# Retention in two-batch steps with routing in three rounds, in a retention-and-experts kernel

## Chip, cores and metric

The kernel runs on one core of a Trainium2 chip, as one launch. The metric is device time in microseconds (us); lower is better. Before the change the median of three runs is 463.68 us (463.49 to 468.06).

## What is computed

A retention layer feeds a mixture of experts. Arrays are float32: 4 batches, 8 heads, 768 positions, 64 features a head; so 3072 tokens of 512 features, 8 experts of 1024 hidden units.

```
for t in range(S):                       # retention, S = 768
    state = gamma * state + outer(k[t], v[t])
    y[t] = scale * (q[t] @ state)
x = y as rows (3072, 512)
logits = x @ w_gate                      # (3072, 8)
expert = argmax(logits); gate = softmax(logits)[expert]
out[row] = gate * (relu(x[row] @ w1[expert]) @ w2[expert])
```

The kernel uses the chunked form of retention. For 128 positions it computes scores (queries times keys, masked to the causal half), the product of the scores with the values, and, from the second chunk on, the product of the queries with a running state of 64x64 per head.

## The kernel before

Four engines follow an order written out by hand: TensorE (PE), VectorE (DVE), ScalarE (ACT) and GpSimd (POOL). SyncE (SP) issues nearly all transfers, in the order in which the program names them. Each engine works through its list without overtaking, so an instruction that waits holds all behind it on its engine.

**Retention, units of one batch.** `steps` (L453) lists 24 units, a unit being one chunk of one batch: for each pair of chunks, for each batch, the even and then the odd chunk. One query tile holds both chunks of a pair, so queries are loaded, scaled and transposed for every second unit. `load` (L456) runs five units ahead on SP, with six buffers for keys and for values. `scale` (L478) multiplies queries and values by decay factors, on POOL except for the first unit. `transpose` (L499) turns keys and queries on PE, and ACT copies them out (L513, L516). `retain` (L520) does a unit: the scores (L528) on PE, their masking on DVE (L530, tile `am`), then for the next unit the transposes, the new state (PE L539, DVE L542), the query-state product (L556), the product of scores and values (L560), and three copies of the result into `xTg` on ACT (L563, L567; for the last unit two of them on DVE, L569). `to_rows` (L571) turns a unit into rows on DVE (L574); `store` (L579) writes four units to the scratch `x_d` with four transfers of 256 KB (L581).

**Routing, six rounds.** After every four units `place` (L584) is started. It is a generator: each `next(rest)` in the loop puts its next piece into the engines' lists. It computes the logits (PE L591), picks each token's expert, ranks the tokens within an expert (PE L624 to L628, `rk`), and builds with one-hot products (`val` L662, `here` L670, PE `found` L677) the table `inv` (L680) of which token stands in which place. The fifth round, after 20 of the 24 units, ends with `sources` (L173) and a gather of the first 256 rows of experts 0 and 1 from `x_d` (L166, POOL): the early rows. The sixth is spread over the first expert's first layer.

**Between retention and the experts.** DVE copies the early rows of expert 0 (`xe`, L741), PE transposes them (L754), and they are copied out as `xTa` (L756, L758). Then come the eight blocks of the first layer for 256 rows (`layer1`, L223; `hTa`), among which the last round's pieces stand (after blocks 0, 1 and 3; `count`, L415, after block 2). The second layer of the early rows is `pair` (L341), a scheme with seven products instead of eight, which needs sums of the hidden values (`halves_of_h`, L248: `he`, two on DVE and two on POOL) and of the weights (`halves_of_w`, L259: `we`, four on DVE). Two of the weight sums stand before the first layer in DVE's list (L760), two after the last round (L772). After that DVE transposes the other rows of expert 0 (`xTa`, L209) and all of expert 1 (`xT1`, L786), and the loop over the experts (L899) starts. It is a chain of PE work to the end.

**Buffers in PSUM.** Eight banks: two for scores (`sc`), one for logits (`lg`), three for transposes, new state and routing (`tr`), two for outputs (`y`).

Of the kernel before, what the change touches and what calls it, by code (L numbers as in the profile page):

```python
# [53 lines left out]
def kernel(  # L54
# [24 lines left out]
    FAR = 1 << 20  # L79
    assert NC == S // P and D == 64 and DM == H * D and N == B * S and NT == B * NC and DM == 512  # L80
# [51 lines left out]
    nc.gpsimd.iota(tile_4, pattern=[[Q, NT]], base=1, channel_multiplier=0, **exact)  # L132
# [6 lines left out]
    acc = rt([P, NC + 1, E], "acc", BF16)  # L139
# [43 lines left out]
    def targets(got, far, name):  # L183
# [5 lines left out]
        nc.vector.tensor_single_scalar(two, at, 2 * Q - 1, op=ALU.bitwise_and)  # L189
        nc.vector.tensor_single_scalar(bt, at, (2 * Q).bit_length() - 1, op=ALU.arith_shift_right)  # L190
        nc.vector.tensor_single_scalar(bt, bt, B - 1, op=ALU.bitwise_and)
        nc.vector.tensor_single_scalar(ct, at, (2 * Q * B).bit_length() - 1, op=ALU.arith_shift_right)
        nc.vector.scalar_tensor_tensor(out=far, in0=two, scalar=float(L), in1=far, op0=ALU.mult, op1=ALU.add)
        nc.vector.scalar_tensor_tensor(out=far, in0=ct, scalar=float(2 * P), in1=far, op0=ALU.mult, op1=ALU.add)
# [220 lines left out]
    def count():  # L415

        cnt = ps("y", 2, "cnt")[:, 0:E]
        nc.tensor.matmul(cnt, lhsT=ones_b, rhs=acc[:, NC, :], start=True, stop=True)
        ne = rt([P, E], "ne")
        nc.vector.tensor_copy(ne, cnt)  # L420
        return ne
# [14 lines left out]
    with ExitStack() as actx:  # L436
# [6 lines left out]
        def warm(width):  # L443
            nc.tensor.matmul(ps("lg", 1, "warm")[:, 0:width], lhsT=idle[:, 0:P], rhs=idle[:, 0:width], start=True, stop=True)
# [6 lines left out]
        xg = [keep.tile([P, B, Q, DT * L], F32, tag=f"xg{i}", name=f"xg{i}") for i in range(2)]  # L451
        xTg = [keep.tile([P, DT, B, P], F32, tag=f"xTg{i}", name=f"xTg{i}") for i in range(2)]
        steps = [(2 * m + e, b) for m in range(NC // 2) for b in range(B) for e in range(2)]  # L453
        qkv, scaled, qT2, front, state = {}, {}, {}, {}, {}

        def load(n):  # L456
            c, b = steps[n]
            got = {}
            for nm, src in (("k", k), ("q", q), ("v", v)) if n else (("q", q), ("k", k), ("v", v)):
                if nm != "q":  # L460
                    got[nm] = att.tile([P, H, D], F32, tag=nm, name=nm, bufs=6)
                    nc.sync.dma_start(got[nm], src[b, :, ts(c, P), :].rearrange("h t d -> t h d"))
                elif c % 2 == 0:
                    got[nm] = att.tile([P, H, 2 * D], F32, tag=nm, name=nm, bufs=3)
                    for hs in (range(2) if n == 0 else [0]):
                        part = ts(hs, HP) if n == 0 else slice(0, H)
                        nc.sync.dma_start(got[nm][:, part, :], src[b, part, ts(c // 2, 2 * P), :].rearrange(
                            "h (t e) d -> t h (e d)", e=2))
            qkv[n] = got

        def heads_first(src, pairs=range(HP), tr=None):
            if tr is None:
                tr = ps("tr", 3, "tr").rearrange("p (a t) -> p a t", a=HP)
            for a in pairs:
                nc.tensor.transpose(tr[:, a, :], src[:, 2 * a : 2 * a + 2, :].rearrange("p h d -> p (h d)"), ident)
            return tr

        def scale(n):  # L478
            c, b = steps[n]
            got = qkv.pop(n)  # L480
            mul = nc.gpsimd if n else nc.vector
            qs = None
            if c % 2 == 0:
                qs = att.tile([P, 2, H, D], F32, tag="qs", name="qs")
# [10 lines left out]
            if n:  # L495
                scale_v()
# [498 lines left out]
```

## Time and profile before

| | |
|---|---|
| three runs | 463.49, 463.68, 468.06 us |
| the profiled execution | 468.13 us, its span 466.4 us |
| mean granted TensorE clock | 0.992 |
| PE busy | 443.3 us, 95% of the span |
| DVE busy | 295.1 us, 63% |
| POOL busy | 244.0 us, 52% |
| ACT busy | 130.5 us, 28% |
| moved by DMA | 72.75 MB, mean 156 GB/s |

A row of the timeline has the start in us from the start of the span, the duration, the engine, the line, the operation, out<-in, the shapes, how many instructions are merged in the row, and in brackets how long the engine had been idle before it and what it had waited for. A table of windows has for each stretch the busy time of each engine with its instructions, the clock that the throttle granted TensorE (PEclk), the busy share of the DMA engines, and what they moved.

### The profile page before, as it was taken

Reading aid. Unit: us, or ns where it says so; the run is one execution under the profiler, and the core shown is the slowest. Engines: PE = TensorE matmul, PEld = TensorE weight load, DVE = VectorE, ACT = ScalarE, POOL = GpSimd, SP = SyncE. Lnnn points to the kernel's source line nnn. Section 1 sums busy time; section 2 is a strip of 40 time slices with the busy share of each in tenths; the row PEclk is TensorE's granted clock in tenths of the full one; section 3 lists DMA queues with packets and bytes.
Section 4 is the critical chain, followed back from the end, with each engine's and each line's share of the span. In section 5 each row is a group of like instructions: output and inputs, shape, how many; then the busy total and the mean of one; then the engine's idle time right before and its main releaser. Section 6 shows DMA issues by size and latency. Waiting matters only on the chain.

```text
span 466.4 us, 9449 instructions
## 1 busy us (share of the span) xinstructions
PE 443.3 (95%) x3550; PEld 354.6 (76%) x3550; DVE 295.1 (63%) x674; ACT 130.5 (28%) x315; POOL 244.0 (52%) x192
## 2 busy tenths in 40 slices
PE   8899999989799999999999999999989999999992
PEld 4778777767567774558977994898889599699772
DVE  4468788798677792842676567257766748744410
ACT  3454444535322020221231132114213212212310
POOL 3772624450304247728924890885389189179311
PEclk9999999999989999999999999999999999999998
DMA  9998999998931089605804532290562415001001
GB/s 202 225 239 202 220 214 225 241 222 268 288 91 42 4 301 386 245 13 215 273 4 183 174 152 82 107 313 7 185 229 87 180 50 214 5 6 63 4 28 49
DMA packets 93543, 72.75 MB, mean 156 GB/s; under 512 B 53482, under 2 KB 78058, under 8 KB 93424
## 3 DMA queue, kind: packets, MB, share of 16 engines
q1 hardware_dynamic: 88160, 58.74, 44.9%
q0 software_dynamic: 5120, 12.60, 7.6%
q8 instruction: 47, 0.77, 0.7%
q14 instruction: 72, 0.59, 0.4%
q10 hardware_dynamic: 144, 0.05, 0.0%
HBM read 60.88 MB, written 14.68 MB: 162 GB/s over the span
## 4 chain that ended last, share of the span: by engine, by line
PE 59%; DVE 5%; issue 1%; ACT 0%; POOLq 0%; DVEq 0%
PE p L303 24%; PE p L349 18%; PE p L236 13%; PE p L223 5%; DVE xT L209 2%; DVE xTa L209 1%; DVE xs L355 0%; PE yp L349 0%; POOLq L991 0%; ACT o L241 0%; ACT o L242 0%; DVE u L355 0%; DVE hT L307 0%; DVE two L189 0%; DVE dst L195 0%
## 5 line engine op out<-in xcount | busy, mean ns | idle before, releaser
L236 PE MATMUL p<-w2t,hT 128*8 128x128 f32 (+6 forms) x496 | 66.5, 361 | 0.0
L236 PEld LDWEIGHTS p<-w2t,hT 128*8 128x8 f32 (+6 forms) x496 | 32.2, 122 | 30.0 <-issue 26.7
L209 DVE STREAM_TRANSPOSE xT<-xs 32x512 f32<-32x512 f32 x64 | 44.9, 702 | 6.2 <-issue 5.1
L394 POOL DMA_INDIRECT out_dram<-o,dst x30 | 29.9, 996 | 28.3 <-ACT o L244 11.8
L166 POOL DMA_INDIRECT xs<-x_d,src x28 | 29.3, 1045 | 29.2 <-DVE gate_e L201 18.0
L530 DVE TENSOR_TENSOR am<-sc,causal 128x512 f32<-128x512 f32 x48 | 30.7, 681 | 17.2 <-PE sc L528 13.7
L209 DVE STREAM_TRANSPOSE xTs<-xs 32x512 f32<-32x512 f32 x48 | 33.7, 702 | 12.1 <-issue 11.3
L487 POOL TENSOR_TENSOR qs<-q,dec 128x512 f32<-128x512 f32 x22 | 22.5, 1044 | 35.0 <-DMA q<-in_q_dram 33.9
L954 POOL COPY turn_of<-t 128x1 f32<-128x1 f32 x6 | 1.1, 182 | 74.2 <-DVE t L289 74.2
L349 PE MATMUL p<-ws,hs 128*128 128x256 f32 x168 | 37.4, 379 | 0.0
L307 DVE TENSOR_TENSOR hT<-p,q 128x196 f32<-128x196 f32 (+5 forms) x72 | 23.9, 359 | 20.8 <-PE p L303 20.0
L303 PE MATMUL p<-t,w1t 128*128 128x196 f32 (+5 forms) x192 | 35.8, 329 | 0.0
L303 PE MATMUL p<-t,s 128*128 128x196 f32 (+5 forms) x192 | 35.8, 329 | 0.0
L349 PEld LDWEIGHTS p<-ws,hs 128*128 128x128 f32 x168 | 31.9, 190 | 4.3
L492 POOL TENSOR_TENSOR vs<-v,dec 128x512 f32<-128x512 f32 x23 | 23.9, 1042 | 21.4 <-DMA v<-in_v_dram 10.2
L265 POOL TENSOR_TENSOR ws<-w2t,ws 128x1024 f32<-128x1024 f32 x14 | 33.1, 2364 | 0.5
L265 POOL TENSOR_TENSOR ws<-w2t 128x1024 f32<-128x1024 f32 x14 | 33.1, 2364 | 0.1
L303 PEld LDWEIGHTS p<-t,w1t 128*128 128x128 f32 x192 | 32.4, 190 | 0.0
L303 PEld LDWEIGHTS p<-t,s 128*128 128x128 f32 x192 | 32.4, 190 | 0.0
L560 PE MATMUL y<-am,vs 128*64 128x128 f32 x384 | 30.5, 285 | 1.8 <-DVE am L530 1.4
L355 DVE SCALAR_TENSOR_TENSOR o<-p,gate,q 128x256 f32<-128x256 f32 x21 | 10.1, 483 | 30.9 <-PE p L349 30.5
L560 PEld LDWEIGHTS y<-am,vs 128*64 128x64 f32 x384 | 22.9, 140 | 7.5 <-DVE am L530 4.4
(205 smaller groups left out, 848.0 us busy)
## 6 DMA issues: line engine op xcount, KB each, us to landing
w1t<-in_moe_w_dram SPq DMA_DIRECT2D x8, 2048.0 KB, 8.1
w2t<-in_moe_w_dram SPq DMA_DIRECT2D x8, 2048.0 KB, 10.8
k<-in_k_dram SPq DMA_DIRECT2D x24, 256.0 KB, 5.3
v<-in_v_dram SPq DMA_DIRECT2D x24, 256.0 KB, 5.7
x_d<-xg SPq DMA_DIRECT2D x24, 256.0 KB, 5.0
q<-in_q_dram SPq DMA_DIRECT2D x11, 512.0 KB, 6.3
q<-in_q_dram SPq DMA_DIRECT2D x2, 256.0 KB, 3.4
out_dram<-o,dst POOLq DMA_INDIRECT x30
```

Source lines behind the costliest of these rows:

```text
L166: nc.gpsimd.indirect_dma_start(out=xs[:, t, :], out_offset=None, in_=x_d[0:rows, :], in_offset=bass.IndirectOffsetOnAxis(ap=idx[:, t : t + ...
L209: nc.vector.transpose(xT[ts(g, L), :, 0 : n * P].rearrange("p a (t r i) -> p r t a i", r=Q, i=L)[:, r, :, :, :], xs[ts(r, L), tiles[0] : t ...
L223: nc.tensor.matmul(hp, lhsT=w1t[:, 0, dt, ts(f, P)], rhs=xT[:, dt, 0:n], start=(dt == 0), stop=(dt == DT - 1))
L236: nc.tensor.matmul(y[j * z : j * z + m, 0:c], lhsT=hT[:, f, t * P + r0 : t * P + r0 + m], rhs=w2t[:, 0, f, ts(j, c)], start=(i == 0), stop ...
L265: by.tensor_tensor(out=ws[i], in0=sums[i][0], in1=sums[i][1], op=ALU.subtract)
L303: nc.tensor.matmul(rows(y), lhsT=a(d, f), rhs=b(d), start=start and d == 0, stop=d == 1, skip_group_check=True)
L307: nc.vector.tensor_tensor(out=to, in0=rows(y), in1=rows(plus), op=ALU.add)
L349: nc.tensor.matmul(y, lhsT=a[:, f, :], rhs=b[:, f, :], start=start and f == 0, stop=f == FH - 1, skip_group_check=True)
L394: done = nc.gpsimd.indirect_dma_start(out=out[:, :], out_offset=bass.IndirectOffsetOnAxis(ap=idx[:, t : t + 1], axis=0), in_=o[:, t, :], i ...
L492: mul.tensor_tensor(out=vs, in0=got["v"], in1=inner(dec[:, ts(NC + c, H)], D), op=ALU.mult)
L530: nc.vector.tensor_tensor(out=am[j], in0=sc[j], in1=middle(causal[:, :], HP), op=ALU.mult)
L560: nc.tensor.matmul(place_of(a, j), lhsT=vs[:, 2 * a + j, :], rhs=am[j][:, a, :], start=(c == 0), stop=True, skip_group_check=True)
```

## The change

A step is now one chunk of two batches; there are 12 steps (`where`), and each phase of a step is done for both batches before the next phase. The order of tokens in `x_d` follows, and with it some index arithmetic (`tile_4`, `targets`).

- The state of two batches is one tile, so its update is one DVE instruction of 128x512; a step's outputs fill two banks and are copied out by three ACT instructions of 512 columns (for the last step one of the three on DVE, behind the copies of `xe`).
- Logits are computed after every step (256 columns instead of 512 for four units) into a kept tile `lg`; one transfer to `x_d` has 128 KB, four a step.
- Routing runs in three rounds, of five, four and three steps (10, 8 and 6 tiles of 128 tokens). The early rows come from the first nine steps; the second round ends in step 11, the last step, and its gather with it.
- The last round stands after blocks 0, 2 and 5 of the first layer, `count` right behind the ranking product, and all four weight sums of `halves_of_w` behind the last round.
- The weights of expert 0 are loaded in steps 9 and 10, ahead of those steps' stores.
- PSUM: four banks for scores and query transposes (`sc`), two for key transposes, logits, state and routing (`tr`), two for outputs.

```diff
+    NEXT = (0, 5, 9, STEPS)
-    acc = rt([P, NC + 1, E], "acc", BF16)
+    acc = rt([P, NR + 1, E], "acc", BF16)
...
+        def turn_q(s, b, parts=1, by=(nc.scalar.copy, nc.scalar.copy)):
+            qs = raw.pop(("qs", s, b))
+            qT2[b] = att.tile([P, HP, P, 2], F32, tag="qT", name="qT")
+            trs = [pairs_of("sc", 4, "trq") for _ in range(2)]
+            for i in range(parts):
+                for e in range(2):
+                    heads_first(qs[:, e, :, :], trs[e], range(i * HP // parts, (i + 1) * HP // parts))
+            for e in range(2):
+                by[e](out=qT2[b][:, :, :, e], in_=trs[e])
+
+        def turn_k(s, b):
+            kT = att.tile([P, HP, P], F32, tag="kT", name="kT")
+            tr = pairs_of("tr", 2, "trk")
+            heads_first(raw["k", s, b], tr)
+            nc.scalar.copy(out=kT, in_=tr)
...
+        def within(s, y, am):
...
+            nc.scalar.copy(out=x[s][:, 0:HB, :, :].rearrange("p a b t -> p b a t"), in_=y[0])
+            for j in range(2):
+                to, got = x[s][ts(j, D), HB:HP, :, :].rearrange("p a b t -> p b a t"), y[1][ts(1 - j, D), :, :, :]
+                if j and s + 1 == STEPS:
+                    nc.vector.tensor_copy(to, got)
+                else:
+                    nc.scalar.copy(out=to, in_=got)
...
+        def logits(s):
+            parts = ps("tr", 2, "parts")[:, 0 : 2 * P]
+            m = P // DT
+            for dt in range(DT):
+                nc.tensor.matmul(parts[ts(dt, m), :], lhsT=wg[:, dt, :], start=True, stop=True,
+                                 rhs=x[s][:, dt, :, :].rearrange("p b t -> p (b t)"))
+            lgT = att.tile([P, 2 * P], F32, tag="lgT", name="lgT", bufs=1)
+            nc.scalar.copy(out=lgT, in_=parts)
+            return lgT
...
+        WHEN = {5: "abc", 6: "ab", 7: "ab", 8: "pa", 9: "ac", 10: "ab", 11: "pa"}
...
+            if s:
+                am = [scores(s, b) for b in range(2)]
+            y = outputs()
+            if where[s][0] or where[s][2]:
+                with_state(s, y)
...
+            if s:
+                lgT = logits(s - 1)
+                if s + 1 < STEPS:
+                    ahead()
+                reduce = logits_of(s - 1, lgT)
+                if s + 1 < STEPS:
+                    ahead_q()
+                step(s, "p")
+                if s + 1 == STEPS:
+                    step(s, "a")
+                to_rows(s - 1)
+                reduce()
+                if s - 1 != NEXT[NR - 1]:
+                    store(s - 1)
+                if s == NEXT[NR - 1]:
+                    wa = [weights1(first, 0)]
+                if s == NEXT[NR - 1] + 1:
+                    wa.append(weights2(first, 0))
+                    store(s - 1)
+                if s in NEXT:
+                    rest = chain(rest, place(NEXT.index(s) - 1))
+                if s + 1 < STEPS:
+                    step(s, "a")
+            next_state(s)
+            step(s, "b")
+            if s + 1 == STEPS:
+                for t in range(HALF):
+                    nc.vector.tensor_copy(xe[:, t, :].rearrange("p (a q l) -> p q a l", q=Q, l=L),
+                                          xs2[0][:, t, :].rearrange("p (q a l) -> p q a l", q=Q, l=L))
+            within(s, y, am)
+            if s == 0:
+                ahead()
+            step(s, "c")
+
+        lgT = logits(STEPS - 1)
+        rest = place(NR - 1)
+        pad_ranks(acc[:, NR - 1, 0:2])
...
-        halves_of_w(wa[1], we, [0, 1])
+        to_rows(STEPS - 1)
+        store(STEPS - 1)
         for f in range(FT):
-            layer1(EARLY, xTa, wa[0], hTa, f, (("sc", 2), ("sc", 2), ("lg", 1), ("tr", 3)))
-            if f in (0, 1, 3):
+            layer1(EARLY, xTa, wa[0], hTa, f, (("sc", 4),))
+            if f == 0:
+                logits_of(STEPS - 1, lgT)()
+                next(rest)
+            if f == 2:
+                next(rest)
+                ne = count()
+            if f == 5:
+                next(rest)
                 next(rest, None)
-            if f == 2:
-                ne = count()
...
-        T = halves_of_w(wa[1], we, [2, 3])
+        T = halves_of_w(wa[1], we)
```

In the loop `scores`, `with_state`, `next_state` and `within` are the four parts of the old `retain`, each for both batches. `ahead` calls `turn_k` and `ahead_q` calls `turn_q`, for both batches of the next step; `logits_of` transposes a step's logits on PE and returns the DVE reduction. The letters in `WHEN` are the places of a step where a piece of a routing round is put: `p` behind the transposes, `a` behind the row transposes, `b` behind the new state, `c` behind the step.

## The prediction, made before the changed kernel was run

> **What bounds the kernel now.** I read the windows first, then the PE timeline, then the DVE and POOL rows between retention and the experts.
>
> ```profile
> core 0: us, PE busy (x) PEld busy (x) DVE busy (x) ACT busy (x) POOL busy (x), PEclk, DMA share, GB/s
> 20.00:124.00 104.00, 99.83 (x1503) 78.88 (x1501) 82.66 (x229) 48.91 (x111) 44.98 (x44) 1.00 0.98 235
> 124.00:134.00 10.00, 7.14 (x59) 4.07 (x57) 5.14 (x13) 2.65 (x6) 1.83 (x2) 0.83 0.36 111
> 134.00:178.00 44.00, 42.46 (x215) 33.23 (x216) 37.00 (x105) 8.28 (x23) 15.32 (x14) 1.00 0.43 142
> 178.00:466.00 288.00, 277.50 (x1608) 227.21 (x1607) 161.71 (x310) 63.31 (x162) 172.49 (x109) 0.99 0.36 128
> ```
>
> PE is busy for 96% of retention, and the DMA share is 0.98: little to win there. The hole is at 124 to 134. Everything behind 178 us is untouched.
>
> ```profile
> 124.40:127.80 3.40, 1.24 (x20) 0.61 (x16) 0.81 (x2) 1.10 (x3) 1.44 (x2) 1.00 0.78 234
> 127.80:131.20 3.40, 3.37 (x20) 2.04 (x20) 1.94 (x4) 0.37 (x1) 0.00 (x0) 0.50 0.06 23
> 131.20:134.60 3.40, 2.73 (x20) 1.61 (x17) 2.99 (x8) 1.17 (x2) 0.00 (x0) 1.00 0.24 57
> ```
>
> A stretch with only 1.24 us of PE work is followed by one at half the clock; 2.73 us of work keeps it full. What released the engines in that hole the profile does not say (its waits read "issue" and "remote").
>
> ```profile
> 45.09 1.16 PE L528 MATMUL sc<-qT,kT 64*128 64x128 f32 x16
> 46.18 0.66 PE L475 MATMUL tr<-ident,k 128*128 128x128 f32 x4
> 46.67 0.44 PE L677 MATMUL found<-val,here 128*128 128x160 bf16 x4
> 47.04 1.06 PE L591 MATMUL parts<-xTg,wg 128*32 128x512 f32 x8
> 48.04 0.68 PE L539 MATMUL new<-vs,k 128*64 128x64 f32 x16
> 48.66 0.67 PE L556 MATMUL y<-qT,state 64*64 64x128 f32 x16
> 49.25 1.09 PE L560 MATMUL y<-am,vs 128*64 128x128 f32 x16
> ```
>
> From start to start these rows price the phases of one batch: scores 1.09, key transposes 0.49 (0.58 where another kind follows), new state 0.61, query-state 0.60, outputs 1.03; query transposes take 0.96 (41.88 to 42.85).
>
> ```profile
> 121.01 1.22 POOL L166 DMA_INDIRECT xs<-x_d,src_e  x1 [12.03 <-DVE src_e L180]
> 131.23 0.76 DVE L741 COPY xe<-xs 128x512 f32<-128x512 f32 x2
> 134.00 2.00 PE L223 MATMUL hp<-xTa,w1t 128*128 128x256 f32 x8 [0.67 <-ACT xTa L756]
> 146.66 1.22 DVE L265 TENSOR_TENSOR we<-w2t,we 128x1024 f32<-128x1024 f32 x1
> 150.06 0.69 DVE L253 TENSOR_TENSOR he<-hTa 128x512 f32<-128x512 f32 x1 [2.18 <-ACT hTa L225]
> 177.81 7.48 PE L223 MATMUL p<-xT,w1t 128*128 128x392 f32 x22 [0.67 <-DVE dst L195]
> ```
>
> After retention the early gather (121.01) is done long before `xe` is copied; the last two weight sums `we` end before the hidden values are ready (DVE idles 2.18). From `he` on DVE runs without a hole to 177.6, and PE has only 0.67 of slack at 177.81: what makes `he` later, makes the end later.
>
> **Part 1, retention.** Work is not removed. At full speed the phases between 20.16 (outputs of the third unit) and 123.39 (scores of the last) sum to 97.0: 21 outputs 21.6, 20 scores 21.8, 20 key turns 10.8, 10 query turns 9.4, 17 states 10.5, 18 query-state 10.8, five rounds of logits 5.0, their turns 2.9, ranks 2.0, `found` 2.2. They took 103.2, so waits cost 6.2.
>
> A new step of two batches: scores 2.18, query-state 1.20, logits 0.55 (half of 1.00 for half the columns, a little more for the start; at most 1.00), keys 1.03, turn of the logits 0.30, new state 1.24, outputs 2.06, sum 8.5; every second step 1.9 more for queries. The waits on `am`, `y` and `state` go: masks (4 x 0.65 on DVE) are done 3.9 into the step, outputs start at 7. What is late next: `tr` has two banks for five users a step. The turn of the logits takes the bank of the first keys and waits for ACT (logits copy 0.37, then keys 0.59): about 0.35. In steps without query turns the new state waits about 0.30 for the second keys. So 9.2 and 10.85. Steps 1 to 10, less the missing query-state of step 2 and state of step 9, take 97.9; two rank products and one `found` of ten tiles 2.2. The last step takes 7.8: scores, query-state and logits to 3.9, turned logits 4.8, `found` of eight tiles 5.7, outputs 7.8. DVE enters it late, as `val` and `here` of eight tiles (2 x 0.83 and 8 x 0.18) stand at the end of step 10: it masks from 3.2 to 5.8, just in time for the outputs.
>
> Start: scores of batch 0 stand at 7.92 as now, but batch 1 needs a second 512 KB query tile. The unit-2 query tile now lands at 13.05 behind 1.8 MB; behind 0.8 MB I take 8.2, then 2.04 on POOL, turns, copies, scores at 12.3; step 1 starts at 18.6. Last outputs end at 18.6+97.9+2.2+7.8 = 126.5. Without any new wait it is 121.0. Now it is 130.3, of which 4.2 is the hole at 124.4 and the half clock behind it; without them 126.1.
>
> Covered: six `place` rounds become three, with half the small DVE instructions (DVE is busy 82.66 of 104); row turns and scalings are the same; logits copies on ACT (48.91 of 104) are shorter. `xs` clears move on POOL, which idles 57%. SP: 24 stores of 256 KB become 48 of 128 KB with the same packets; a store now waits for `to_rows` in mid-step with the next loads behind it. Loads are ordered two steps ahead and used some 13 us later, against 5 to 6 to land; if that cover went, a step would grow to SP's issue time, 4 x 0.99 and 5 x 1.2 = 10.0, against 10.0 on average: nothing to 4 us in all. The two weight loads go out at about 107, behind the store of step 8, and are needed at 135 and 151; that of w2 leaves before the store of step 9, which nothing waits for until the last gather.
>
> The rows of `x_d` show 256 KB stores landing 2.8 to 5.8 us after their issue, several in flight, so a transfer's own latency overlaps the next one's. [...]
>
> **Part 2, from the last outputs to the first layer.** The early round now ends inside the last step: `found` 5.7 after its start, `inv` 0.35, `sources` 0.85, gather issued at 7.2. What that gather waits for in `x_d`, the stores up to step 8, is long done. POOL issues the two tiles of expert 0 1.5 us apart; now the first bytes move 2.5 us after the first issue and both tiles have landed after about 5.2, beside the weight load; without it I take 4.4 as the lower bound. DVE copies `xe` at 11.6 to 12.4, and only behind that comes its share of the last outputs, for which the logits and all of PE wait: 0.76+0.7, so 13.0 to 13.9. PE has been idle since 7.8. Then 2.95 to the first layer (131.25 to 134.0 is 2.75 now): 15.7 to 16.8, or 7.9 to 9.0 after the last outputs, middle 8.5. Now it is 134.0-130.3 = 3.7, undisturbed 4.0. Cost +4.5.
>
> **Part 3, first layer to the second product of `pair`.** Block 2 ends at 5.6 (counted from the first layer), ranks 6.0. `count` stands right behind and waits for four DVE instructions (own, rank, seen, acc): 1.0 of PE idle. DVE builds `val` and `here` for six tiles until 11.2; `found` is ordered behind block 5, 12.4 to 13.2; `inv`, `sources`, gates and `arm` end at 16.2 (now 145.6-134.0 = 11.6). Then four weight sums instead of two, 4 x 1.23 = 4.9, to 21.1, and `he` to 22.55. Now `he` ends at 151.48, so 17.5. PE's second product waits from 18.4 to 22.6, where it now starts at 17.6. Cost +5.0 (4.3 if ranks are quicker, 5.7 if `found` is later), and it reaches 177.8 in full. The last gather is issued at 14.5 (now 10.2) behind the store of step 11, whose four transfers leave at about 1 and take 3.4 us of SP and some 5 to land; its rows are due only behind `he`.
>
> **Part 4, the clock.** Two new holes in PE, of 5 and 4 us. By the row above a stretch of 3.4 us with little work is followed by 3.4 at half, 1.7 lost where PE is dense. Around the first hole one or two such stretches, 2.0; after the second part of one, 1.0. Together 3.0, bounds 0 and 3 x 1.7 = 5.1.
>
> [...] The row shows the drop with no single gap over 1.25. [...]
>
> **The sum.** Undisturbed: +0.4 +4.5 +5.0 +3.0 = +12.9. The profiled execution (468.13, span 466.4 and 1.7 around it) is 4.45 above the median 463.68; its hole and half clock explain 4.2. From it: 468.13 -3.8 +4.8 +5.0 +3.0 = 477.1. From the median: 476.6, which I take.
>
> **Rivals.** A: the new waits on `tr` do not come and retention ends at 121.0, 5.1 sooner; with 1.5 for the clock 463.7-5.1+4.5+5.0+1.5 = 469.6. For it: waits now are 6.2 in all. Against: two banks, five users. B, the other side: a change of phase on PE costs more than its row shows, and 66 fewer of them pay. The row shows 0.09 (key turns 0.58 against 0.49), 5.9 in all: 470.7. It must be 0.125 to be within 1% of before and 0.27 (17.6 us) to be faster by over 1%: 459. Against it: scores to keys shows 0. C: SP becomes the bound of retention, +4: 481. D: nothing to measure, if A and B come together without the clock: 463.7-5.1-5.9+4.5+5.0 = 462.
>
> **How the numbers follow.** Forecast 0.70 (471 to 481, slower), A 0.14 (0.09 slower, 0.05 within 1%), B beyond its point 0.05 (faster), C 0.05 (slower), D 0.06 (within). The low end is A with the smallest gather (-0.6) and layer term (-0.7) and no clock: 466.8; the high end is 476.6 with clock +2.1 and the upper ends +0.6, +0.7 and 1.5 for waits: 481.5. Over 1% (4.6 us, about what a measurement can tell from no change): slower 0.84, within 0.11, faster 0.05.
>
> **What would show it.** Step starts 9.2 and 10.85 apart; `xe` waiting for its gather and the last logits for `xe`; `he` 22 us after the first layer's start; PEclk near 0.5 after two holes. It is wrong if the last step ends before 121, if `xe` does not wait, or if PE's second product of `pair` starts under 19 us after the first layer.

## The result, and the profile after

The changed kernel takes 469.96 us, median of nine runs (468.25 to 475.07), beside 463.68 for the kernel before (nine runs, 462.93 to 468.06): ratio 1.0132, 95% interval 1.0092 to 1.0172. It is slower, as forecast, and inside the whole range (466.8 to 481.5) but under the 471 to 481 of the forecast itself: by 6.3 us and not by 12.9. In two more comparisons the ratio was 1.0104 (1.0049 to 1.0158) and 1.0216 (1.0139 to 1.0293), with four runs of the changed kernel each. Ratios are taken from undisturbed executions, medians from all. In all three comparisons the kernel before had 463 to 465 us; beside a kernel before at 468 to 469 us, which other comparisons had, the changed kernel was not run.

The profiled execution took 471.93 us, its span is 470.2 and the mean clock 0.976. Its windows, cut where its own stages end (columns as before):

```profile
core 0: us, PE busy (x) PEld busy (x) DVE busy (x) ACT busy (x) POOL busy (x), PEclk, DMA share, GB/s
20.00:120.00 100.00, 93.97 (x1602) 78.30 (x1598) 67.13 (x154) 45.15 (x84) 45.40 (x43) 1.00 1.01 238
120.00:132.00 12.00, 3.80 (x19) 2.00 (x17) 4.22 (x12) 1.49 (x3) 3.88 (x4) 0.64 0.64 206
132.00:184.00 52.00, 46.42 (x218) 36.05 (x219) 38.47 (x107) 8.36 (x24) 15.41 (x14) 0.92 0.35 114
184.00:470.00 286.00, 277.12 (x1608) 227.18 (x1606) 166.94 (x310) 65.08 (x162) 172.80 (x108) 0.99 0.36 128
```

PE is busy for 94 us in retention where it was for 100 before, and the stretch behind it has 12 us with 3.8 us of PE work, at a clock of 0.64 (before: 10 us with 7.1, at 0.83). The rows of the early rows, with the same groups as those shown of before:

```profile
119.66 1.22 POOL L169 DMA_INDIRECT xs<-x_d,src_e  x1 [10.25 <-DVE src_e L183]
...
125.76 0.43 DVE L803 COPY xe<-xs 128x512 f32<-128x512 f32 x1 [4.95 <-DMA xs<-x_d,src_e]
126.83 0.43 DVE L803 COPY xe<-xs 128x512 f32<-128x512 f32 x1 [0.64 <-DMA xs<-x_d,src_e]
127.28 0.68 DVE L575 COPY xT<-y 64x512 f32<-64x512 f32 x1
```

The gather is issued 0.4 us before the last outputs end, DVE waits 4.95 us for it, and behind `xe` stands DVE's share of the last outputs (`xT`). The first layer's first block at half clock, the second product of `pair` and the start of expert 1, from PE's timeline:

```profile
132.10 3.78 PE L226 MATMUL hp<-xTa,w1t 128*128 128x256 f32 x8 [0.68 <-ACT xTa L823]
...
156.20 7.27 PE L352 MATMUL yp<-we,he 128*128 128x256 f32 x24 [3.40 <-DVE he L257]
...
183.57 1.88 PE L226 MATMUL p<-xT,w1t 128*128 128x392 f32 x5 [0.91 <-ACT o L247]
```

The first block took 2.00 before. The waits of PE from 14 to 165 us:

```profile
PE parts L598 <- DVE xT L575: 7.4, 1, 7.4
PE yp L352 <- DVE he L257: 3.4, 1, 3.4
PE trk L488 <- DMA k<-in_k_dram: 3.2, 3, 1.4
PE cnt L421 <- DVE acc L652: 0.9, 1, 0.9
...
PE new L553 <- ACT kT L507: 0.8, 3, 0.3
```

(Total, times, longest.) Every wait that the prediction announced is there; the one on a key load is new.

Milestones in us of the span. The third column is the kernel before without its early gather, explained below, and the fourth the changed kernel on that same chip.

| | before | after | before_nog2 | after3 |
|---|---|---|---|---|
| last outputs end | 130.30 | 120.09 | 126.79 | 119.05 |
| first layer starts | 134.00 | 132.10 | 130.49 | 130.70 |
| second product of `pair` | 151.63 | 156.20 | 148.13 | 154.75 |
| first product of expert 1 | 177.81 | 183.57 | 174.34 | 181.88 |
| span | 466.4 | 470.2 | 462.9 | 467.4 |

So after against before: retention -10.2, to the first layer +8.3, to the second product +6.5, to expert 1 +1.2, behind that -2.0.

### The profile page after: what moved, and what is told of

Same layout as the page of the kernel before. It is cut to its first block, busy times and chain, and to the rows that moved or that the text cites. A ratio compares the mean times of both kernels' runs of the same rounds, so it can differ in the third digit from the quotient of the medians.

```text
span 470.2 us, 9505 instructions
## 1 busy us (share of the span) xinstructions
PE 437.0 (93%) x3595; PEld 355.7 (76%) x3595; DVE 283.9 (60%) x597; ACT 127.1 (27%) x283; POOL 245.3 (52%) x192
## 4 chain that ended last, share of the span: by engine, by line
PE 78%; DMA 6%; DVE 6%; issue 5%; ACT 2%; SPq 1%; POOL 1%; POOLq 0%; ACTq 0%; DVEq 0%
PE p L306 24%; PE p L352 16%; PE p L239 12%; PE p L226 6%; PE sc L520 3%; PE y L569 3%; PE hp L226 3%; PE yp L352 3%; DMA k<-in_k_dram 3%; PE trq L488 2%; PE new L553 2%; ACT kT L507 1%; DMA q<-in_q_dram 1%; PE y L540 1%; DMA xs<-x_d,src_e 1%
## 5 line engine op out<-in xcount | busy, mean ns | idle before, releaser
L482 POOL TENSOR_TENSOR vs<-v,dec 128x512 f32<-128x512 f32 x23 | 24.1, 1064 | 35.6 <-DMA v<-in_v_dram 29.7
L306 PE MATMUL p<-t,s 128*128 128x196 f32 (+5 forms) x192 | 35.8, 329 | 0.0
L306 PE MATMUL p<-t,w1t 128*128 128x196 f32 (+5 forms) x192 | 35.8, 329 | 0.0
L477 POOL TENSOR_TENSOR qs<-q,dec 128x512 f32<-128x512 f32 x22 | 22.6, 1050 | 20.2 <-DMA q<-in_q_dram 17.4
L306 PEld LDWEIGHTS p<-t,s 128*128 128x128 f32 x192 | 32.4, 190 | 0.0
L306 PEld LDWEIGHTS p<-t,w1t 128*128 128x128 f32 x192 | 32.4, 190 | 0.0
L310 DVE TENSOR_TENSOR q<-p,q 128x196 f32<-128x196 f32 (+5 forms) x48 | 16.5, 360 | 17.9 <-PE p L306 12.9
L352 PE MATMUL p<-w2t,hT 128*128 128x256 f32 x112 | 27.0, 382 | 0.2 <-ACT q L367 0.2
```

The costliest lines, as they stand in the source:

```text
L306: nc.tensor.matmul(rows(y), lhsT=a(d, f), rhs=b(d), start=start and d == 0, stop=d == 1, skip_group_check=True)
L310: nc.vector.tensor_tensor(out=to, in0=rows(y), in1=rows(plus), op=ALU.add)
L352: nc.tensor.matmul(y, lhsT=a[:, f, :], rhs=b[:, f, :], start=start and f == 0, stop=f == FH - 1, skip_group_check=True)
L477: by.tensor_tensor(out=qs[:, e, part, :], in0=got[:, part, ts(e, D)], op=ALU.mult, in1=inner(dec[:, ts(2 * where[s][0] + e, H)][:, part], D))
L482: by.tensor_tensor(out=vs, in0=raw.pop(("v", s, b)), op=ALU.mult, in1=inner(dec[:, ts(NC + 2 * where[s][0] + where[s][2], H)], D))
```

## The experiments

Five comparisons, each on one chip with the kernel before beside it.

| comparison | median of before (runs) | medians (runs), ratio to before |
|---|---|---|
| 1 | 468.64 (19) | xe_last 468.21 (10), 0.9999; sums_back 470.44 (10), 1.0002; mixed 478.52 (4), 1.0236 |
| 2 | 464.90 (23) | after2 469.70 (4), 1.0104; early10 464.64 (10), 0.9994; all3 460.53 (8), 0.9872; before_nog 464.48 (8), 1.0001 |
| 3 | 468.92 (22) | after_warm 472.75 (9), 1.0082; all4 466.61 (12), 0.9951 |
| 4 | 462.96 (21) | after3 472.04 (4), 1.0216; before_nog2 463.29 (10), 1.0000; after_warm8 466.17 (6), 1.0081; all3b 461.35 (10), 0.9905 |
| 5 | 467.76 (13) | before5 468.00 (10), 1.0006; all5 462.90 (4), 0.9894 |

The kernel before was also profiled once each as before2 (comparison 1), before3 and before4 (comparison 3). Its median differs between comparisons by up to 6 us, so times are compared only within one of them.

### What a change of kind costs on PE

The theory is that PE pays at each change from one kind of product to another, and that retention got shorter because a step has fewer of them; the rival, that waits vanished. `mixed` brings back two changes a step:

```diff
...
+            y = outputs()
             if s:
-                am = [scores(s, b) for b in range(2)]
-            y = outputs()
-            if where[s][0] or where[s][2]:
+                am = []
+                for b in range(2):
+                    am.append(scores(s, b))
+                    if where[s][0] or where[s][2]:
+                        with_state(s, y, [b])
+            elif where[s][0] or where[s][2]:
                 with_state(s, y)
```

> The changed kernel with scores and query-state product in turns: scores of batch one, query-state of batch one, then the same for batch two. The same PE instructions, with two more changes of kind in each of ten steps. If retention got shorter because a change of kind costs PE about 0.2 us where the same kind would go on after 0.06 to 0.1, the ten steps get longer by 0.2 to 0.35 us each, the last outputs end 2 to 3.5 us later than at 120.0, and the time rises by as much. Rival, that the gain came from waits on masks, outputs and states that vanished: the masks of the second batch come 0.5 us later, still 2 us ahead of their use, so nothing moves by more than 0.5 us in all.

Ratio 1.0236 (1.0163 to 1.0308). The same even step, first of the changed kernel and then of `mixed`:

```profile
47.59 2.06 PE L520 MATMUL sc<-qT,kT 64*128 64x128 f32 x32
49.58 1.10 PE L540 MATMUL y<-qT,state 64*64 64x128 f32 x32
50.61 0.64 PE L598 MATMUL parts<-xT,wg 128*32 128x256 f32 x8
51.18 1.27 PE L488 MATMUL trk<-ident,k 128*128 128x128 f32 x8
52.56 0.44 PE L607 MATMUL lgp<-ident,lgT 128*128 128x128 f32 x2
53.27 1.15 PE L553 MATMUL new<-vs,k 128*64 128x64 f32 x32 [0.27 <-ACT kT L507]
54.23 1.95 PE L569 MATMUL y<-am,vs 128*64 128x128 f32 x32
56.10 2.06 PE L520 MATMUL sc<-qT,kT 64*128 64x128 f32 x32
```

```profile
47.12 1.16 PE L520 MATMUL sc<-qT,kT 64*128 64x128 f32 x16
48.21 0.90 PE L540 MATMUL y<-qT,state 64*64 64x128 f32 x16
49.05 1.16 PE L520 MATMUL sc<-qT,kT 64*128 64x128 f32 x16
50.14 0.67 PE L540 MATMUL y<-qT,state 64*64 64x128 f32 x16
50.74 0.64 PE L598 MATMUL parts<-xT,wg 128*32 128x256 f32 x8
...
56.23 1.16 PE L520 MATMUL sc<-qT,kT 64*128 64x128 f32 x16
```

From scores to logits 3.02 us become 3.62 with the same work, and the step takes 9.11 instead of 8.51. Not all of that is the price of two changes. In the shown step ACT still copies the last outputs out of `y` when the first state product starts, and half of that product must wait until 48.41; its row takes 0.90, where the second takes 0.67. The table marks no wait so short. In steps 1, 6 and 10 this copy is done in time. The copies in the step shown and in step 6, and PE in step 6:

```profile
47.24 1.17 ACT L577 COPY xT<-y 64x512 f32<-64x512 f32 x2 [0.29 <-PE y L569]
...
66.86 1.17 ACT L577 COPY xT<-y 64x512 f32<-64x512 f32 x2 [0.29 <-PE y L569]
67.16 1.16 PE L520 MATMUL sc<-qT,kT 64*128 64x128 f32 x16
68.25 0.67 PE L540 MATMUL y<-qT,state 64*64 64x128 f32 x16
68.84 1.16 PE L520 MATMUL sc<-qT,kT 64*128 64x128 f32 x16
```

The logits follow at 70.53, so 3.37 us; in steps 1 and 10 it is 3.38 and 3.37. Two more changes cost 0.35, about 0.18 each, and the other 0.25 of the shown step is the wait on `y`. The expectation had 0.2 to 0.35 a step and 2 to 3.5 us at the last outputs; it is 0.35 to 0.60, and the last outputs end at 123.93, 3.8 later than in the changed kernel, which did not run in this comparison. The theory holds, and the rival, under which nothing moves by more than 0.5, does not.

The changed kernel's own step agrees. By the one-batch rows its four doubled phases hold eight changes; three are left (scores to state product, state product to logits, outputs to scores), and the four phases take 0.83 us less than the doubled rows, 0.17 for each change that is gone. Between the new state and the outputs, which follow each other now, no tile changes: both have 128\*64. The phases here have five tiles (64\*128, 64\*64, 128\*32, 128\*128, 128\*64 in the rows), and the price just given, 0.17 to 0.18 us, stands between phases of different tiles.

### The way from retention to the experts

`xe_last` moves the two copies `xe` behind the last outputs in DVE's list:

```diff
+            within(s, y, am)
             if s + 1 == STEPS:
                 for t in range(HALF):
...
-            within(s, y, am)
```

> The changed kernel with the two copies of the early rows behind the last outputs' DVE copy instead of ahead of it. If the order on DVE holds up the logits: the last logits start within 1.5 us of the last outputs (121 instead of 128), and the first layer starts when the early rows have landed, copied, been transposed and copied again, 129.5 to 131 instead of 132.1; the time falls by 1 to 3 us. Rival, that the gather's latency alone sets the first layer: the logits move forward, the first layer does not move by more than 0.7 us, and the time stays within 1 us.

The logits start at 118.06, right behind the outputs, but the first layer only at 126.17: it waits for the gather. From the last outputs to the first layer it is 8.0 us instead of 12.0, so the order on DVE cost about 4. Ratio 0.9999 (0.9968 to 1.003); the changed kernel did not run in this comparison, so what the edit is worth in time is not measured.

`sums_back` puts two of the four weight sums ahead of the first layer again (`halves_of_w(wa[1], we, [0, 1])` before the blocks, `[2, 3]` behind).

> The changed kernel with two of the four weight sums again ahead of the first layer in DVE's list. DVE idles 3.8 us there, so they are hidden. If the four sums behind the last round delay the second product of the pair: the hidden sums start 2.45 us sooner (152.2 instead of 154.6), PE's wait of 3.40 us ahead of the second product shrinks to about 1, the stretch of half clock at 157.5 goes, and the time falls by 2.5 to 4 us. Rival, that the last round's gather or PE holds that product: nothing moves by more than 0.7 us.

Ratio 1.0002 (0.9969 to 1.0034). PE's wait on `he` (3.4) is gone, two of 1.3 and 0.9 stand in its place; first layer to second product 21.0 instead of 24.1. The 2.5 to 4 us of time that were expected can't be read for the same reason; in this profile PE waits 2.23 us for the weights `w2t` ahead of expert 1.

`early10` has the edit of `xe_last`, and finishes the second routing round at the end of step 10, so that its gather is issued earlier. `all3` adds the edit of `sums_back` and puts `count` behind block 3 instead of block 2; `all3b` is `all3` on another chip.

```diff
-        WHEN = {5: "abc", 6: "ab", 7: "ab", 8: "pa", 9: "ac", 10: "ab", 11: "pa"}
+        WHEN = {5: "abc", 6: "ab", 7: "ab", 8: "pa", 9: "ac", 10: "pacd"}
...
             step(s, "c")
+            step(s, "d")
```

> The changed kernel once more, beside the kernel before and the variants on one chip. Theory: retention is 10 us shorter, the way from the last outputs to the first layer 8 longer, the first layer to the second product of `pair` 6.5 longer. The kernel before took 463.68 us on the chip of the first comparison and 468.64 on that of the first variants. If the chip slows both kernels alike, after is 1.013 times before here as well (about 475 where before is 468.6); if the slower chip's extra is bound to something only one of them does, the ratio changes. Last outputs end at 119 to 120.5, first layer at 131 to 132.5 in either case.

> Two edits: the second routing round is finished at the end of step 10, not inside step 11, and the copies `xe` stand behind DVE's copy of the last outputs. Theory (the first layer is late because the gather is issued only 0.5 us before the last outputs end): gather issued at about 116 instead of 119.7, landed at 122 to 123, first layer at 125 to 127 instead of 132, against 126 to 130 with the copies moved alone; time 5 us under the changed kernel, 466 to 469 beside a changed kernel of 471 to 474. Rival (the hole comes with the gather wherever it stands: PE, DVE and ACT stand still while it runs): the last step becomes longer by 3 to 4 us, last outputs end at 121.5 to 124, first layer not before 129, time within 2 us of the changed kernel.

> The edits of the run before (second round finished in step 10, `xe` behind the last outputs), and in the first layer two of the four weight sums ahead of it and the count behind block 3 instead of block 2. Theory: first layer at 125 to 127, second product of `pair` 18.5 to 20.5 behind it (24.1 in the changed kernel, 21.0 with the sums alone moved), one stretch of half clock or none behind the outputs: 10 us less than the changed kernel, 461 to 465 beside one of 471 to 474, and 1 to 1.5 % under the kernel before. Rival (what is won before the experts is given back there, as the two sums ahead brought only 0.03 % against before): under 4 us below the changed kernel.

> The version with the second round finished early, `xe` behind the last outputs, two weight sums ahead of the first layer and the count behind block 3, once more on another chip, where it had 460.5 us beside 464.9 and 469.7. Theory: 8 to 10 us under the changed kernel here too. Rival (it drops to the level of the version with its wait taken away, 466.6 beside 468.9, where a hole before `xe` brought 10 us of half clock): 4 to 6 us under the changed kernel.

In these profiles `xe` follows the last outputs without a wait for the gather, and no half clock follows before the second product; `early10` has its first layer at 126.66 and is 5 us under the changed kernel beside it (first layer 131.03), as expected; its gather is issued at 117.3 and not at 116, and its last outputs end at 122.34, since step 10 got longer. `all3` has ratio 0.9872 (0.982 to 0.9924), `all3b` 0.9905 (0.9861 to 0.9949): faster than both kernels in two comparisons. By the medians of all executions, which spread over 10 to 13 us, it is 0.9% and 0.3% under the kernel before. In the profiled execution of `all3` (470.28 us) PE waits 2.24 and 4.11 us on its way to expert 1, in that of `all3b` (460.46) it does not. Its own fault is in step 10, where DVE's work for the round goes ahead of the logits' sum (profile of `all3b`):

```profile
108.78 0.44 PE L607 MATMUL lgp<-ident,lgT 128*128 128x128 f32 x2
111.34 1.74 PE L553 MATMUL new<-vs,k 128*64 128x64 f32 x32 [2.12 <-DVE lg L608]
112.80 3.06 PE L569 MATMUL y<-am,vs 128*64 128x128 f32 x32
```

The outputs there take 3.06 instead of 1.95, as half a clock follows the wait (0.50 from 111.66 to 115.08). `all4` takes the wait away: the sum goes first, and `found` stands behind the first scores of step 11.

> The last version (second round finished early, `xe` behind the last outputs, two weight sums ahead of the first layer, count behind block 3) with its own wait taken away: in step 10 the logits' sum goes first on DVE, and `found` of the second round stands behind the first scores of step 11. That wait held PE for 1.8 and 2.9 us in two executions, with a stretch of half clock behind the longer. Theory: last outputs end 1 to 2 us sooner (120 to 121.5), gather issued at 116.5 to 117.5, first layer at 124.5 to 126; median 458.5 to 460 where the version before had 460.5 beside a kernel before of 464.9. Rival (the gather's landing sets the first layer, whatever PE does): first layer not sooner, time the same within 0.5.

The last outputs do end sooner, at 120.17, yet the first layer starts at 127.46 and runs at half clock. PE now has nothing to do for 2.5 us while the gather lands:

```profile
119.26:122.67 3.41, 1.47 (x22) 0.81 (x18) 0.59 (x3) 1.17 (x2) 2.71 (x3) 1.00 0.90 255
122.67:126.08 3.41, 2.46 (x11) 1.56 (x12) 1.86 (x7) 0.37 (x1) 0.00 (x0) 0.50 0.77 253
126.08:129.50 3.42, 2.74 (x9) 1.99 (x8) 3.33 (x5) 0.59 (x1) 0.00 (x0) 0.50 0.20 41
129.50:132.91 3.41, 3.41 (x11) 2.68 (x10) 1.82 (x7) 0.63 (x2) 0.00 (x0) 0.50 0.50 113
```

The first layer is not sooner, as the rival said: the wait taken from PE came back behind it, with 10 us of half clock. What holds the first layer is less plain than the rival has it. ACT and DVE stand still as well, for 1.94 and 2.82 us that the profile calls "remote" and "issue", and `xe` follows at 123.20 without a wait for the gather. `all5` fills this hole with three products whose result is never read.

> The version all4 with three filling products (0.88 us each by the run with fourteen, so 2.6) between the last outputs and the rest of the last logits, where PE waited 2.5 us and 10 us of half clock followed; their result is never read. Theory: no half clock before the experts, logits no later, first layer 1 us sooner, second product 18.3 behind it instead of 21.0; time 3 us under the 0.995 of before that all4 had: 0.985 to 0.990. Rival (the eight blocks at half clock are hidden beside DVE's chain): 0.993 to 0.997.

No half clock before the experts, first layer at 127.16 (not sooner), second product 18.3 behind it instead of 21.0, ratio 0.9894 (0.9842 to 0.9947), as expected. From the last outputs to the second product it is 24.5 us instead of 28.3. `all3` and `all5` both have little left for PE to wait for when the gather lands: in the one a wait further ahead has put PE's work later, in the other idle products fill the hole. Which is faster is not known, as they did not run in one comparison.

### The half clock, and the hole in the kernel before

`after_warm` and `after_warm8` are the changed kernel with such filling products in its own hole:

```diff
+        busy = ps("sc", 4, "busy")
+        for i in range(8):
+            nc.tensor.matmul(busy, lhsT=idle[:, 0:P], rhs=idle, start=True, stop=True)
         lgT = logits(STEPS - 1)
```

> The changed kernel with fourteen products of 128x512 (zero use: their result is never read) in PE's list between the last outputs and the last logits, about 7 us of PE work in a hole of 7.2 to 7.4 us. Theory (the half clock behind the hole costs 4 to 5 us): no stretch of half clock before 155, the logits start at the same time, first layer 1 us sooner, eight blocks 15.3 instead of 18.0 to 18.4 us, second product of `pair` 3 us sooner; time 3 to 5 us less. Rival (DVE's chain of the last routing round sets the end in any case, and the slower blocks are hidden beside it): second product under 1 us sooner, time within 1 us of the changed kernel.

Fourteen took 12.28 us and not 7, so they pushed the first layer back to 135.34. With eight:

> The changed kernel with eight filling products (12.28 us for fourteen, so 7.0) between the last outputs and the last logits, whose result is never read. Theory: no half clock before 155, the logits start no later than in the changed kernel by more than 0.5, first layer at 130.5 to 131.5, second product 21.5 to 22 behind it (21.7 with fourteen, at full clock; 24.1 and 23.6 without): 3 us sooner, time 2 to 4 us under the changed kernel. Rival: given back behind the second product, time within 1 us of the changed kernel.

> The changed kernel beside the runs below on one chip. Its medians were 469.96 and 469.7 us on chips where the kernel before had 463.68 and 464.9. Theory (before's hole with the gather is what tells the chips apart, and the changed kernel hides it in its wait for the gather): 469 to 472 here too, whatever before has; a ratio of 1.000 to 1.005 if before has 468 to 469 here, 1.010 to 1.014 if it has 463.5 to 465. Rival (some chips are slower for both): the ratio stays 1.010 to 1.014 on every chip.

Windows of `after3`, then of `after_warm8`, along their windows of 3.41 us:

```profile
118.37:121.78 3.41, 1.24 (x18) 0.58 (x12) 1.41 (x3) 1.02 (x2) 2.55 (x3) 1.00 1.09 353
121.78:125.19 3.41, 0.00 (x0) 0.00 (x0) 0.43 (x1) 0.00 (x0) 1.67 (x2) 0.50 1.07 332
125.19:128.61 3.42, 1.73 (x8) 0.85 (x9) 1.60 (x5) 0.37 (x1) 0.00 (x0) 0.50 0.25 98
128.61:132.02 3.41, 2.74 (x10) 2.16 (x9) 1.90 (x3) 0.58 (x1) 0.00 (x0) 0.50 0.01 2
132.02:135.43 3.41, 3.41 (x10) 2.68 (x10) 0.43 (x2) 0.38 (x1) 0.00 (x0) 0.50 0.69 151
```

```profile
118.18:121.60 3.42, 3.42 (x17) 1.66 (x14) 1.19 (x3) 0.81 (x2) 2.77 (x3) 1.00 0.46 115
121.60:125.00 3.40, 3.40 (x9) 1.52 (x8) 0.57 (x2) 0.00 (x0) 1.45 (x2) 1.00 1.04 311
125.00:128.43 3.43, 2.94 (x19) 1.24 (x17) 2.15 (x7) 0.58 (x2) 0.00 (x0) 1.00 0.16 66
```

First layer at 128.86 instead of 130.70, second product at 150.60 instead of 154.75, expert 1 at 177.68 instead of 181.88. The last outputs of `after_warm8` ended 0.4 sooner, so the half clock behind the first hole costs 3.8 us up to expert 1. The medians are 466.17 and 472.04; the four runs of `after3` lie at 469 and at 475, so 2.9 to 5.9 us. `after3` was to decide between two views of the chips, but the kernel before had 462.96 beside it, where both views expect a ratio of 1.010 to 1.014; it was 1.0216.

All five profiles of the kernel before show the hole of the prediction's second fence, at the same place, while the gather runs.

> The kernel before, one look. Two of its executions in the profile showed a hole of 4 us in PE, DVE and ACT at 124 to 128 and half a clock behind it, and took 468.1 and 469.2 us; the copy without the early gather showed none and took 464.7, but its median was that of the kernel before. Theory (the hole comes in some executions only, and the median is one without it): in one of two more looks there is none, last outputs end at 126 to 127 and the time is 463 to 465. Rival (it comes always with the gather): both looks have it, last outputs end at 129.5 to 130.5.

> The kernel before, profiled and timed. Theory (the hole belongs to some executions, one stretch of 3.41 us at half clock each: 0.992 and less of mean clock, without it 0.995 and more, and 3 to 4 us between the two groups): if the profiled execution shows the hole it lies 3 to 5 us over the lower group of the timed ones; if it is within 1.5 us of the lower group, last outputs end at 126 to 127 and there is no stretch of half clock before the end. Rival (the hole is in every execution): the profiled execution shows it and is within 1.5 us of the median.

In four of the five one stretch of half clock follows; in `before5` none does, with the same idle time in PE (1.20 and 0.71 us):

```profile
122.27:125.68 3.41, 2.21 (x36) 1.84 (x36) 1.05 (x3) 0.37 (x1) 2.68 (x3) 1.00 0.88 303
125.68:129.10 3.42, 2.41 (x32) 1.56 (x32) 1.91 (x3) 1.04 (x3) 0.32 (x1) 1.00 0.50 147
```

Here the hole is split between two windows, 2.21 and 2.41 us of work; in the first profile of the kernel before it fell into one, with 1.24. The execution took 467.66 us, about its median (468.00): on this chip the hole is in the usual execution, as the rival said.

`before_nog` and `before_nog2` leave the early gather out (two lines of `place`); the early rows are computed from zeros.

> The kernel before without its early gather: the two transfers of early rows are left out and the rows are computed from zeros. All else stays, `xe` included. Theory (the hole of 4 us in PE at 124.4 comes with the gather, since it stands in two executions while the gather runs): no hole, last outputs end at 125.5 to 127, first layer at 129.5 to 131, no half clock; time 4 us less. Rival (the hole has another cause, in the last unit's own order of work): last outputs end at 129.5 to 130.5 as now.

> The kernel before without its early gather (the early rows are computed from zeros). Theory (the hole comes with the gather): where before's median is 468 to 469, this one is 4 us under it, 464 to 465; where before's is 463.5 to 465, the same as before. Rival (the hole and the chip's level have nothing to do with each other): within 1 us of before on a chip of 468 to 469.

Neither has the hole; the last unit of `before_nog2` runs through:

```profile
123.17 1.16 PE L528 MATMUL sc<-qT,kT 64*128 64x128 f32 x16
124.26 0.67 PE L556 MATMUL y<-qT,state 64*64 64x128 f32 x16
125.19 1.59 PE L560 MATMUL y<-am,vs 128*64 128x128 f32 x16 [0.27 <-DVE am L530]
126.81 1.98 PE L591 MATMUL parts<-xTg,wg 128*32 128x512 f32 x8
```

So the hole comes with the gather. From the start of the last scores to the first layer the kernel before takes 10.6 to 10.8 us with a stretch of half clock and 9.65 without (`before5`); both copies without the gather take 7.32. The hole costs 2.3 us there and the half clock 1.0. But both medians equal that of the kernel before beside them, 464.48 to 464.90 and 463.29 to 462.96. The kernel before was at 462.96 to 464.90 in three comparisons and at 467.76 to 468.92 in three others, and in the comparison of the result its profiled execution lay 4.4 us over its median. All this fits a hole that is usual on some chips and rare on others. It is not shown: no profile of the kernel before without the hole was had on a fast chip, and the copy without the gather wasn't tried on a slow one.

## Why the prediction was wrong, step by step

The direction and every wait that was announced were right; the size failed, and it failed first in **Part 1**. One sign of being wrong that the prediction named came, the last step ending before 121: it ended at 120.09.

- **Failed: "A new step of two batches: scores 2.18, query-state 1.20 ... new state 1.24, outputs 2.06", and with it the price 0.09 of rival B.** Each start-to-start row of one batch holds one change of kind, and Part 1 doubled it with the row, so that a step paid eight changes where three are left. Measured in the step shown above: 1.99, 1.03, 0.96 (after 0.27 of wait), 1.87, together 0.83 less. The steps are 8.51 and 9.92 where 9.2 and 10.85 were said, with the 0.35 and the 0.30 of waiting on `tr` both there (1.38 from keys to `lgp`, 0.27 at `new`). Over steps 1 to 10 that is 7.7 us; ranks, `found` and a wait for the round (`told`) took 1.6 instead of 2.2, and waits on key loads made two steps longer by 2.6: 94.4 from step 1's start to the last step's, where 100.1 was forecast. The price 0.09 came from the one pair of rows between which the change is cheap, key turns before another kind. The reading that 96% busy leaves "little to win there" fell with it: changes of kind count as busy time (the 3.02 us from scores to logits in the changed kernel and the 3.37 in step 6 of `mixed` are both without idle time). None of the four phases stood beside its like in the trace of before, but its rows have five tiles and five changes a unit, and four key turns took 0.49 before `found`, which has their tile, and 0.58 before another: something to price could be seen.
- **Start and last step.** Step 1 starts at 18.63 (18.6 said). The last step took 7.1, not 7.8. Last outputs 120.09 instead of 126.5.
- **"Without them 126.1".** Without hole and half clock the kernel before ends retention at 126.8 and 127.7 (the two copies without gather). The number was 0.7 and 1.6 off (hole and half clock are 3.3 of it, not 4.2), and its ground was not right: the hole is no accident of one execution, it stands in five of five. That the median leaves it out too may be so in some comparisons (above), and is not shown.
- **Part 2, 8.5.** It was 12.0 (11.65 in `after3`): outputs to the second half of the logits 7.9 by the late `xe`, as described, with the gather landing 6.1 and 7.2 us after its first issue instead of 4.4 to 5.2, and half the clock in the rest.
- **Part 3, 22.6.** 24.1 with half clock and 21.7 without (`after_warm8`): `count` waits 0.9 (1.0 said), PE 3.4 for `he` (4 said).
- **Part 4, 3.0, bounds 0 to 5.1.** 3.8 for the first hole alone, where 2.0 was said, and one stretch more behind the second hole, of 3.4 us (0.5 from 157.4 on, after a window with 1.2 us of PE work). The row "2.73 us of work keeps it full" holds at full clock only: in `after3` 2.74 us of work at half clock is followed by another half window.
- **"It reaches the end in full".** Not quite: behind expert 1's start the changed kernel takes 286.6 us where the kernel before takes 288.6, and 1.9 of the difference are waits of PE in the experts' products (L303, 2.2 before; L306, 0.3 after) that the profile calls "issue". Why they went is open.

The rivals: A falls, since the waits on `tr` came; that its 469.6 is nearly the measured 469.96 is luck. B was nearest: 8.4 us (7.7, and 0.7 in the last step) over the 66 changes it counted is 0.13 each, at its point for "within 1%"; the result is a little slower because the first hole cost more. C did not come: no wait on SP's queue but the key loads, 0.7 to 3.2 us a profile. Nor did 24 more stores show as a cost: the 48 stores of 128 KB, which SP issues, landed 3.8 us after their issue (median), the 24 of 256 KB before 5.0.

Together, from 476.6: -7.7 in the steps, -0.6 in ranks and `found`, -0.7 in the last step and +2.6 by key loads, +3.5 in Part 2 and +1.5 in Part 3 less the 3.0 that stood in Part 4, +1.2 to expert 1, -2.0 behind it: 471.4, against 471.93 profiled and 469.96 in the median.

## What to carry to other kernels

Price a phase of products as its first start to the last start, plus one change to the next kind; when two like phases are put together, one change goes (about 0.18 us here), and the five a step that went here came to 8 us, nearly 2% of the time. Where a gather feeds the next stage, its issue time plus its landing (6.1 and 7.2 us for the two tiles here) can set that stage: find what PE can do meanwhile before the waits ahead of it are taken away. A hole in PE cost itself and the half windows behind it here (2.3 and 1.0 us in the kernel before), so useful work, or even idle products, laid into it can be worth more than its length, as in `all5` (3.8 us up to the second product, for a hole of 2.5).

## What the runs showed of the hardware that was not expected

- A change of tile shape on PE cost about 0.18 us (0.83 us a step for five changes, 0.35 for two in steps 1, 6 and 10 of `mixed`). Between neighbours of one tile none shows: the first output starts 0.02 us behind the last product of the new state (54.23), the first state product 0.20 behind the last scores (49.58).
- The clock goes by windows of 3.41 us: half the clock lasts 3.41 us in the kernel before (127.79 to 131.20) and 13.65, four windows, in the changed kernel (123.26 to 136.91) and in `after3` (121.78 to 135.43); in the changed kernel 20.48 at full, six windows, and 3.41 at half follow. The windows fall at other places of the kernel in other executions: one starts at 124.37 in the first profile of the kernel before, at 122.27 and 125.68 in `before5`. Those with up to 1.47 us of PE work in the rows above were followed by half the clock, those with 2.21 and 2.41 were not; once at half, 1.73 and 2.74 did not end it. Busy time alone does not decide: a window with 1.65 at full clock was followed by full clock (`early10`, from 110.37), one with 1.73 at half by half again (`after3`, from 125.19). Nor was the window ahead of the half clock idle in the kernel before: it held 1.24 us of work.
- While the early gather landed, engines stood still with nothing to wait for in the profile ("issue", "remote"): in the kernel before DVE for 3.52 us and PE for 1.25 and 0.71, in `all4` DVE for 2.82, PE for 2.50 and ACT for 1.94, in `all5` DVE for 2.65. Without the gather none does (`before_nog`, where every wait of DVE and PE has a releaser); in `all3b`, with it, PE does not either (its waits from the last outputs to the first layer are 0.84, 0.42 and 0.67, all with a releaser). What they wait for is not settled.
- A filling product of 128x512 took 0.88 us (fourteen in 12.28), where 0.5 had been expected. A 128x256 product of the first layer takes 0.50 (a block is four, in 2.00 us); the profile shows each of these products as two.
